# Eight units of an expert each, of 128 to 448 tokens, in place of eleven units of one or two blocks

## The chip, the core and the metric

The kernel runs on one core of a Trainium2 chip. The metric is the device time of one launch in microseconds, here the median of the runs shown. One execution was profiled; the rows below are of that execution, and the times in them count from the start of its span.

## The reference

Three stages, in float32. Attention with a window of 32 and 32 global tokens gives 2176 rows of 512 features. A router sends each row to one of 8 experts. A dense layer follows.

```python
logits = x @ w_gate                      # (2176, 512) @ (512, 8)
expert_idx = np.argmax(logits, axis=1)
for e in range(8):
    mask = expert_idx == e
    h = np.maximum(x[mask] @ w1[e], 0.0)   # 512 -> 1024
    out[mask] = gate_w[mask, None] * (h @ w2[e])   # 1024 -> 512
h = out @ w_in                           # 512 -> 2048
g = np.where(h >= 1, h, np.where(h <= -1, 0.0, (h + 1) ** 2 / 4))
result = g @ w_out                       # 2048 -> 512
```

With the reference's inputs (its default seed) the experts get 422, 331, 253, 249, 220, 149, 434 and 118 rows.

## The kernel before

Attention runs first, and the router's counts of rows come out at its end. 128 rows of expert 0 are handled early, between the router's steps, as plain float32 matmuls (`zz`: tiles `zh` and `yp`, with the raw weights `w1r`, `w2r` as an operand). Expert 0 so has 294 rows left, 2048 in all.

Those are cut into blocks of 128 rows. VectorE computes a table of blocks (`code`, `sc`, one-hot `ohh`), TensorE turns it into row numbers (`ip`, then `idx`), and POOL gathers a block's rows from DRAM by an indirect DMA (`gather`, tile `xgb`). Blocks are taken in units: eight pairs of blocks of one expert, and three single blocks, eleven units (`UNITS`, `run(list(range(11)), 0)`). With these inputs 19 blocks hold rows, and the 19 of the eleven units are always computed.

For each unit in turn:

- `x_t` turns each block on TensorE (four 128x128 transposes, tile `xTp`, pool of three banks of PSUM); ScalarE writes a rounded part (`xTh`) and VectorE the rest (`xTl`), both in F32R.
- `l1_pair` is the first layer: for each of 8 slices of the hidden layer, 4 slices of the features and 3 products of parts (`mm3`: high x high, high x low, low x high), one matmul with 256 columns, the pair's rows. 96 matmuls, tile `hp`. ScalarE and VectorE take `hp` to `hTh` and `hTl`. `l1_single` has the weights as the moving operand instead: 24 matmuls of 512 columns, after which the hidden layer is turned on TensorE too.
- `l2` is the second layer: for each block 8 x 3 matmuls of 512 columns (tile `yp`), the hidden layer as the stationary operand. ScalarE scales the block by the gate's weight and POOL scatters it to `ys` in DRAM.

The weights come in as raw float32 (`load_raw`, issued by SP), and `split_w` makes two F32R parts of each of the 8 slices: ScalarE the rounded part (`w1h`, `w2h`), VectorE the rest (`w1l`, `w2l`), 128x1024 elements each. The split of `w2` goes on during a unit's first layer, that of the next unit's `w1` during its second; a slice's next load is issued as soon as it is split. A unit whose expert is the same as the last one's skips its loads.

The order on TensorE, ScalarE, VectorE and SP is that of the code (`manual_schedule`). POOL's is chosen by the scheduler. The program branches once at the start of the units, to a path for more blocks than these:

```python
    with tc.If(slow > 22):
    ...
    block_table()
    run(list(range(11)), 0)
```

After the last unit the dense layer runs from `ys`: `y_tile` turns its rows (three of the seventeen already within the last units), then `fh` and `o` are its matmuls. Its weights are also split, in small steps (`w_step`), the first three sets during the units.

## Time and profile before

| | |
|---|---|
| median of 3 runs | 776.61 us (775.6 to 777.12) |
| profiled execution | 772.4 us, span 770.6 us |
| TensorE busy | 739.3 us, 96% |
| VectorE, ScalarE, POOL busy | 519.4, 361.2, 127.7 us |
| units of the experts | 148.86 to 374.69 us |
| dense layer | from 374.69 us |

A busy time is the sum of the stretches in which an engine had an instruction under way. Matmuls overlap in part, so a group's count times its mean duration is more than the time it holds TensorE; the distance between starts is what counts. Float32 matmuls leave two records each in the trace.

### The profile page before, as it was taken

How to read it: one execution, taken by the hardware profiler on the slowest of the kernel's cores; microseconds unless marked ns; L12 is line 12 of the kernel's file. 1: busy time of each engine (PE TensorE's matmuls, PEld its weight loads, DVE VectorE, ACT ScalarE, POOL GpSimd, SP SyncE). 2: the span in 40 equal slices, each digit the busy share in tenths (PEclk: the TensorE clock that was granted, in tenths of full speed). 3: DMA queues.
4: the chain of work that ended last, by engine and by line, in shares of the span. 5: the costliest groups of instructions: out<-in, count | busy, mean ns of one | idle time of the engine just before them, and what ended most of it. 6: DMA issues, size and time to landing. Idle time of an engine off the chain costs nothing.

```text
span 770.6 us, 16283 instructions
## 1 busy us (share of the span) xinstructions
PE 739.3 (96%) x6524; PEld 642.7 (83%) x6539; DVE 519.4 (67%) x989; ACT 361.2 (47%) x776; POOL 127.7 (17%) x164
## 2 busy tenths in 40 slices
PE   8889878999999999999999999999999999999996
PEld 4666647689899899899899899989989999999984
DVE  4778865578776866956477777757775787545443
ACT  4667653357665656754355553323432432322221
POOL 4345432242221221201100000000000000001112
PEclk9999999999999999999999999999999999999998
DMA  9677952298968966902223211110210100001111
GB/s 300 214 241 244 320 163 85 64 349 277 358 198 270 352 198 236 347 29 83 95 89 101 91 56 54 56 55 1 98 66 1 55 1 1 1 6 64 55 41 69
DMA packets 41954, 103.77 MB, mean 135 GB/s; under 512 B 6798, under 2 KB 11278, under 8 KB 39824
## 3 DMA queue, kind: packets, MB, share of 16 engines
q1 hardware_dynamic: 37312, 88.48, 34.5%
q0 software_dynamic: 4560, 14.19, 4.9%
q8 instruction: 53, 0.87, 0.5%
q14 instruction: 29, 0.24, 0.1%
HBM read 93.45 MB, written 14.18 MB: 140 GB/s over the span
## 4 chain that ended last, share of the span: by engine, by line
PE 80%; issue 7%; DMA 6%; DVE 3%; POOL 1%; SPq 0%; ACT 0%; POOLq 0%; DVEq 0%; ACTq 0%
PE fh L937 7%; PE fh L938 7%; PE fh L939 7%; PE o L938 7%; PE o L939 7%; PE o L937 7%; PE yp L939 5%; PE yp L937 5%; PE yp L938 4%; PE hp L939 4%; PE hp L938 4%; PE hp L937 4%; DMA xgb<-xs,zidx 4%; PE ps_o L300 2%; PE sp L222 2%
## 5 line engine op out<-in xcount | busy, mean ns | idle before, releaser
L1125 DVE SCALAR_TENSOR_TENSOR r<-r 128x384 f32<-128x384 f32 (+1 forms) x96 | 51.4, 536 | 119.8 <-ACT r L1124 119.6
L1127 ACT ACTIVATE gh<-g 128x384 fp32r<-128x384 f32 (+1 forms) x96 | 48.9, 509 | 125.9 <-DVE g L1126 125.9
L1124 ACT ACTIVATE r<-fh,half 128x384 f32<-128x384 f32 (+1 forms) x96 | 54.1, 564 | 114.4 <-PE fh L939 114.3
L939 PE MATMUL o<-wh,gl 128*128 128x512 f32 x272 | 107.5, 395 | 0.0
L937 PE MATMUL o<-wh,gh 128*128 128x512 f32 x272 | 107.4, 395 | 0.0
L938 PE MATMUL o<-wl,gh 128*128 128x512 f32 x272 | 107.2, 394 | 0.0
L938 PE MATMUL fh<-yl,wh 128*128 128x384 f32 (+1 forms) x320 | 104.3, 326 | 0.0
L937 PE MATMUL fh<-yh,wh 128*128 128x384 f32 (+1 forms) x320 | 104.3, 326 | 0.0
L939 PE MATMUL fh<-yh,wl 128*128 128x384 f32 (+1 forms) x320 | 104.2, 326 | 0.0
L1178 POOL DMA_INDIRECT out_dram<-acc,rid x17 | 16.5, 972 | 368.2 <-DVE acc L1176 366.7
L937 PE MATMUL hp<-xTh,w1h 128*128 128x256 f32 x256 | 72.5, 283 | 0.8 <-DVE ei L877 0.8
L939 PE MATMUL hp<-xTh,w1l 128*128 128x256 f32 x256 | 72.4, 283 | 0.0
L938 PE MATMUL hp<-xTl,w1h 128*128 128x256 f32 x256 | 72.4, 283 | 0.0
L938 PEld LDWEIGHTS fh<-yl,wh 128*128 128x128 f32 x320 | 60.0, 188 | 3.6 <-DVE rid L835 0.2
L937 PEld LDWEIGHTS fh<-yh,wh 128*128 128x128 f32 x320 | 60.1, 188 | 3.5
L939 PEld LDWEIGHTS o<-wh,gl 128*128 128x128 f32 x272 | 51.1, 188 | 12.4 <-DVE gl L1133 0.4
L937 PE MATMUL yp<-w2h,hTh 128*128 128x512 f32 x152 | 60.4, 398 | 0.0
L939 PEld LDWEIGHTS fh<-yh,wl 128*128 128x128 f32 x320 | 60.1, 188 | 0.0
L939 PE MATMUL yp<-w2h,hTl 128*128 128x512 f32 x152 | 59.6, 392 | 0.0
L938 PE MATMUL yp<-w2l,hTh 128*128 128x512 f32 x152 | 59.3, 390 | 0.0
L938 PEld LDWEIGHTS o<-wl,gh 128*128 128x128 f32 x272 | 51.1, 188 | 7.9
L937 PEld LDWEIGHTS o<-wh,gh 128*128 128x128 f32 x272 | 51.1, 188 | 7.8
(234 smaller groups left out, 1570.2 us busy)
## 6 DMA issues: line engine op xcount, KB each, us to landing
w1r<-in_w SPq DMA_DIRECT2D x44, 512.0 KB
w2r<-in_w SPq DMA_DIRECT2D x44, 512.0 KB
wraw<-in_wf SPq DMA_DIRECT2D x16, 1024.0 KB
ks<-in_k SPq DMA_DIRECT2D x16, 400.0 KB
v<-in_v SPq DMA_DIRECT2D x16, 384.0 KB
yr<-ys SPq DMA_DIRECT2D x17, 256.5 KB
qp<-in_q SPq DMA_DIRECT2D x16, 256.0 KB
xs<-xr SPq DMA_DIRECT2D x8, 512.0 KB
```

The costliest lines, as they stand in the source:

```text
L222: nc.tensor.matmul(sps[2 * c + z][a * WIN:(a + 1) * WIN, i, :], lhsT=q[r, j * WIN:(j + 1) * WIN], rhs=k_at(k, r, j), start=False, stop=(i ...
L300: nc.tensor.transpose(o[:, i, :], p[:, i, :], ident)
L937: nc.tensor.matmul(o, lhsT=ah, rhs=bh, start=first, stop=False)
L938: nc.tensor.matmul(o, lhsT=ah, rhs=bl, start=False, stop=False)
L939: nc.tensor.matmul(o, lhsT=al, rhs=bh, start=False, stop=last)
L1124: nc.scalar.activation(r[:, 0:w], o[:, 0:w], AF.Relu, bias=half, scale=0.5)
L1125: nc.vector.scalar_tensor_tensor(r[:, 0:w], r[:, 0:w], 1.0, r[:, 0:w], ALU.min, ALU.mult)
L1127: nc.scalar.activation(gh[:, 0:w], g[:, 0:w], AF.Copy)
L1178: w = nc.gpsimd.indirect_dma_start(out=out, out_offset=bass.IndirectOffsetOnAxis(ap=rid[:, tt:tt + 1].bitcast(U32), axis=0), in_=a, in_off ...
```

## The change

One unit for each expert. The experts are ranked by their number of rows (expert 0 first, then the others from the largest down), and rank k has the fixed capacity `CAPS[k]`: 320, 448, 384, 256, 256, 256, 192 and 128 rows. `ORDER` is the order in which the ranks are computed: 320, 448, 384, 128, 256, 192, 256, 256; these are units 0 to 7. Where an expert has more rows than its capacity, a new slow path (`overflow`) handles the rest after a branch.

- `l1_wide` streams a unit's whole capacity in one matmul: 96 matmuls of as many columns as the unit has rows (the unit of 128 keeps `l1_single`).
- A capacity that is no multiple of 128 has a last block of 64 rows. Its hidden layer stays in float32 (`hq`), and its second layer is 16 plain float32 matmuls of 256 columns with the raw `w2r`, on two 128x64 tiles of the array, `o[0:64]` and `o[64:128]`. That block comes first in `l2`, and `w2r` is loaded anew only after it.
- The blocks of a unit's second layer follow one another instead of alternating.
- There are five gather buffers instead of four, and `x_t` turns up to four blocks. The table has 19 entries instead of 24 and takes fewer operations. Each unit loads its weights without a condition. The buffers of wide units lie in those of the dense layer's weights, whose first loads come later.

```diff
-NB = 24
+CAPS = (320, 448, 384, 256, 256, 256, 192, 128)
+ORDER = (0, 1, 2, 7, 3, 6, 4, 5)
+BLOCKS = [(k, 128 * i, min(128, CAPS[k] - 128 * i)) for i in range(4) for k in range(8) if CAPS[k] > 128 * i]
+BLOCKS.sort(key=lambda b: (b[1] > 0, b[2] < 128))
+NB = len(BLOCKS)
+NX = 16
...
-    UNITS = []
-    for z in range(4):
-        UNITS += [(4 * z, 4 * z + 1), (4 * z + 2, 4 * z + 3), (16 + z,)]
-    UNITS += [(20,), (21,), (22,), (23,)]
+    UNITS = [[i for i, b in enumerate(BLOCKS) if b[0] == k] for k in ORDER]
+    for u in UNITS:
+        u.sort(key=lambda i: BLOCKS[i][1])
     xslot = {}
-    for j, u in enumerate(UNITS):
-        for z, i in enumerate(u):
-            xslot[i] = 2 * (j % 2) + z if j < 11 else 2 + j % 2
+    for n, i in enumerate(sum(UNITS, [])):
+        xslot[i] = (0, 1, 4, 2, 3)[n % 5]
     xg = {}
 
     def gather(i):
-        t = xgb[xslot[i]]
-        nc.gpsimd.indirect_dma_start(out=t, out_offset=None, in_=xs,
-                                     in_offset=bass.IndirectOffsetOnAxis(ap=idx[:, i:i + 1].bitcast(U32), axis=0))
+        t, r = xgb[xslot[i]], BLOCKS[i][2]
+        nc.gpsimd.indirect_dma_start(out=t[0:r], out_offset=None, in_=xs,
+                                     in_offset=bass.IndirectOffsetOnAxis(ap=idx[0:r, i:i + 1].bitcast(U32), axis=0))
         xg[i] = t
...
+    gather(UNITS[0][0])
+    gather(UNITS[0][1])
...
-    xTh, xTl = (mp.tile([128, 4, 256], F32R, name=f"xT{z}") for z in "hl")
+    xgb.append(mp.tile([128, XW], F32, name="xgb4"))
+    gather(UNITS[0][2])
+    xTn = [mp.tile([128, 4, 256], F32R, name=f"xT{z}") for z in "hl"]
+    xTw = [wp.tile([128, 1024], I64, tag="wraw", name="xTw", bufs=2).bitcast(F32R)[:, 0:4 * max(CAPS)].rearrange("p (k c) -> p k c", k=4)
+           for z in range(2)]
     hTh, hTl = (mp.tile([128, 8, 256], F32R, name=f"hT{z}") for z in "hl")
+    hTx = [wp.tile([128, 8, 128], F32R, tag=f"w{z}0", name="hTx") for z in "hl"]
+    hq = {}
...
+    def x_turn2(j, z, tag="xT"):
+        i = UNITS[j][z]
+        return turn(xg[i], tag, BLOCKS[i][2])
+
     def x_parts(j, z, p):
         i = UNITS[j][z]
-        parts(p, xTh[:, :, z * 128:(z + 1) * 128], xTl[:, :, z * 128:(z + 1) * 128])
-        V.tensor_copy(gt[xslot[i]], xg[i][:, DM:XW])
+        r = BLOCKS[i][2]
+        parts(p[:, :, 0:r], *(x[:, :, z * 128:z * 128 + r] for x in xT(j)))
+        V.tensor_copy(gt[i][0:r], xg[i][0:r, DM:XW])
+        if r < 128:
+            nc.gpsimd.tensor_copy(gt[i][r:2 * r], xg[i][0:r, DM:XW])
 
     def x_t(j):
-        for z, i in enumerate(UNITS[j]):
-            x_parts(j, z, turn(xg[i]))
+        for z in range(len(UNITS[j])):
+            x_parts(j, z, x_turn2(j, z))
 
     def mm3(o, ah, al, bh, bl, first, last):
         nc.tensor.matmul(o, lhsT=ah, rhs=bh, start=first, stop=False)
         nc.tensor.matmul(o, lhsT=ah, rhs=bl, start=False, stop=False)
         nc.tensor.matmul(o, lhsT=al, rhs=bh, start=False, stop=last)
...
-    def l1_pair(nxt):
-        for g in range(4):
-            o = ps.tile([128, 512], F32, tag="h", name="hp", bufs=3)
-            for u in range(2):
-                f = slice((2 * g + u) * 128, (2 * g + u + 1) * 128)
+    def l1_wide(j, nxt):
+        n = CAPS[ORDER[j]]
+        u = 2 if n <= 256 else 1
+        xh, xl = xT(j)
+        if halved(j):
+            hq[j] = wp.tile([128, YW], F32, tag="yr", name="yr", bufs=4)[:, 0:DM].rearrange("p (f c) -> p f c", f=8)
+            nxt = None
+        for g in range(8 // u):
+            o = ps.tile([128, 512], F32, tag="h", name="hp", bufs=3)[:, 0:u * n]
+            for v in range(u):
+                f = slice((u * g + v) * 128, (u * g + v + 1) * 128)
                 for k in range(4):
-                    mm3(o[:, u * 256:(u + 1) * 256], w1h[k][:, f], w1l[k][:, f], xTh[:, k, :], xTl[:, k, :], k == 0, k == 3)
-            h, l = (t[:, 2 * g:2 * g + 2, :].rearrange("p f c -> p (f c)") for t in (hTh, hTl))
-            nc.scalar.activation(h, o, AF.Relu)
-            V.scalar_tensor_tensor(l, o, 0.0, h.bitcast(F32), ALU.max, ALU.subtract)
-            if g:
-                split_w(2, g - 1, nxt)
+                    mm3(o[:, v * n:(v + 1) * n], w1h[k][:, f], w1l[k][:, f], xh[:, k, 0:n], xl[:, k, 0:n], k == 0, k == 3)
+            o = o.rearrange("p (f c) -> p f c", f=u)
+            e = slice(u * g, u * g + u)
+            m = n // 128 * 128
+            to = [(0, min(m, 256), hTh[:, e, 0:min(m, 256)], hTl[:, e, 0:min(m, 256)])]
+            if m > 256:
+                to.append((256, m, hTx[0][:, e, :], hTx[1][:, e, :]))
+            for a, b, h, l in to:
+                nc.scalar.activation(h, o[:, :, a:b], AF.Relu)
+            if m < n:
+                nc.scalar.activation(hq[j][:, e, :], o[:, :, m:n], AF.Relu)
+            for a, b, h, l in to:
+                V.scalar_tensor_tensor(l, o[:, :, a:b], 0.0, h.bitcast(F32), ALU.max, ALU.subtract)
+            if g * u >= 2 and g * u % 2 == 0:
+                split_w(2, g * u // 2 - 1, nxt)
...
-        o = [ps.tile([128, 512], F32, tag="y", name="yp", bufs=2) for _ in sl]
         if nxt is not None:
             for k in range(2 if len(sl) == 1 else 0, 4):
                 split_w(1, k, nxt2)
         if table:
             positions()
         ahead = nxt is not None and len(UNITS[nxt]) == 1
-        for k in range(4):
-            for z in range(2):
-                f = 2 * k + z
-                for t in range(len(sl)):
-                    c = slice(t * 128, (t + 1) * 128)
-                    mm3(o[t], hTh[:, f, c], hTl[:, f, c], w2h[k][:, z, :], w2l[k][:, z, :], f == 0, f == 7)
-            if k == 0 and 8 <= j < 11:
-                y_tile(j - 8, ps.tile([128, 4, 128], F32, tag="xT", name="xTp", bufs=3), yg, j - 8)
-            if ahead and k < 3:
-                split_w(2, k, nxt2)
-        if not ahead and len(sl) == 2:
-            w_step(5, 3)
-        for t, i in enumerate(sl):
-            g = gt[xslot[i]]
+        todo = list(enumerate(sl))
+        if halved(j):
+            todo.insert(0, todo.pop())
+        for n, (t, i) in enumerate(todo):
+            r = BLOCKS[i][2]
+            o = ps.tile([128, 512], F32, tag="y", name="yp", bufs=2)
+            for k in range(4):
+                for z in range(2):
+                    f = 2 * k + z
+                    if r == 128:
+                        mm3(o, *hT(f, t), w2h[k][:, z, :], w2l[k][:, z, :], f == 0, f == 7)
+                        continue
+                    for q in range(2):
+                        nc.tensor.matmul(o[64 * q:64 * q + 64, 0:256], lhsT=hq[j][:, f, :], rhs=w2r[k][:, z, 256 * q:256 * q + 256],
+                                         start=(f == 0), stop=(f == 7))
+                if n == 0 and k == 0 and 5 <= j < 8:
+                    y_tile(j - 5, ps.tile([128, 4, 128], F32, tag="xT", name="xTp", bufs=3), yg, j - 5)
+                if ahead and n == len(sl) - 1 and k < 3:
+                    split_w(2, k, nxt2)
+            if r < 128 and nxt is not None:
+                for k in range(4):
+                    load_raw(2, k, nxt)
+            if n == 0 and not ahead and j > 3:
+                w_step(6, 3)
+            g = gt[i]
...
+    def run():
+        js = list(range(len(UNITS)))
+        for i in UNITS[1]:
+            gather(i)
         for k in range(4):
-            split_w(1, k, None)
-        x_t(j)
-
-    def run(js, table):
-        if len(js) > 1:
-            for i in UNITS[js[1]]:
-                gather(i)
-            for k in range(4):
-                load_raw(1, k, js[1])
-        for n, j in enumerate(js):
-            nxt, nxt2 = ((js + [None, None])[n + z] for z in (1, 2))
+            load_raw(1, k, 1)
+        for j in js:
+            nxt, nxt2 = (n if n < len(UNITS) else None for n in (j + 1, j + 2))
+            single = len(UNITS[j]) == 1
+            if j == 4:
+                load_y(0)
+                load_y(1)
+            if j == 7:
+                for t in range(3, 6):
+                    load_y(t)
+            l1_single(j, nxt, nxt2) if single else l1_wide(j, nxt)
+            if nxt is not None and not single:
+                x_t(nxt)
             if nxt2 is not None:
                 for i in UNITS[nxt2]:
                     gather(i)
-            single = len(UNITS[j]) == 1
-            if j == 7:
-                load_y(0)
-                load_y(1)
-            if j == 10:
-                for t in range(3, 6):
-                    load_y(t)
-            l1_single(j, nxt, nxt2) if single else l1_pair(nxt)
-            if nxt is not None and not single:
-                x_t(nxt)
-            if j == 8:
+            if j == 5:
                 load_y(2)
-            if j == 0:
+            if j == 3:
                 while wq[0][1] is load_w:
                     f, op = wq.pop(0)
                     op(f)
-            l2(j, nxt, nxt2, j == table)
-
-    def first(j):
-        for kind in (1, 2):
+            l2(j, nxt, nxt2, j == 0)
...
+    with tc.If(slow > 0):
+        overflow()
     block_table()
-    run(list(range(11)), 0)
+    run()
     mo.close()
```

On TensorE, at the end of unit 0's first layer and the start of its second, where the rows of unit 1 are turned (`xTp` is the turned block, `xgb` the gathered one, `yr` holds the hidden layer of the half block). Before:

```order
L939 MATMUL hp<-xTh,w1l_2994 128x256
L920 MATMUL xTp<-ident,xgb_91 128x128 [waits DMASW6_49]
L920 MATMUL xTp<-ident,xgb_91 128x128 x3
L920 MATMUL xTp<-ident,xgb_92 128x128 [waits DMASW7_49]
L920 MATMUL xTp<-ident,xgb_92 128x128 x3
L937 MATMUL yp<-w2h_2995,hTh 128x512 [waits Activation_49]
L938 MATMUL yp<-w2l_2999,hTh 128x512 [waits DVE_49]
```

Now:

```order
L929 MATMUL hp<-xTw,w1l_2984 128x320
L903 MATMUL xTp<-ident,xgb_95 128x128 [waits DMASW0_49]
L903 MATMUL xTp<-ident,xgb_95 128x128 x3
L903 MATMUL xTp<-ident,xgb_96 128x128 [waits DMASW1_49]
L903 MATMUL xTp<-ident,xgb_96 128x128 x3
L903 MATMUL xTp<-ident,xgb_93 128x128 [waits DMASW4_49]
L903 MATMUL xTp<-ident,xgb_93 128x128 x3
L903 MATMUL xTp<-ident,xgb_94 128x64 [waits DMASW5_49,DVE_49]
L903 MATMUL xTp<-ident,xgb_94 128x64 x3
L1010 MATMUL yp<-w2r_89,yr 64x256 [waits DMAHW4_49]
L1010 MATMUL yp<-w2r_89,yr 64x256 x3
L1010 MATMUL yp<-w2r_90,yr 64x256 [waits DMAHW5_49]
```

Four blocks are turned instead of two, the fourth with a wait on VectorE, and the second layer starts with the float32 matmuls of the half block.

On POOL, from the first gathers to the branch at the start of the units (`TENSOR_LOAD nbi` reads the branch's condition). Before:

```order
L686 DMA xgb_89<-xs,idx 128x514 [waits DMAHW2_49,DMAHW1_49,DMAHW7_49,DMAHW0_49,DVE_49]
L686 DMA xgb_90<-xs,idx 128x514
L535 DMA ys<-y,zpos 2176x513 [waits DVE_49,Activation_49]
L1067 TENSOR_LOAD nbi [waits DVE_49]
L1069 COMPARE_AND_BRANCH
```

Now:

```order
L694 DMA xgb_93<-xs,idx 128x514 [waits DMAHW2_49,DMAHW1_49,DMAHW7_49,DMAHW0_49,DVE_49]
L694 DMA xgb_94<-xs,idx 128x514
L694 DMA xgb_2993<-xs,idx 64x514
L920 COPY gt<-xgb_2993 64x2 [waits DMASW3_49,Pool_49]
L694 DMA xgb_93<-xs,idx 128x514 [waits DMASW1_49,DVE_49,PE_49]
L694 DMA xgb_94<-xs,idx 64x514 [waits DMASW2_49,DVE_49,PE_49]
L694 DMA xgb_2993<-xs,idx 128x514 [waits DVE_49,PE_49,Pool_49]
L545 DMA ys<-y,zpos 2176x513 [waits DVE_49,Activation_49]
L920 COPY gt<-xgb_94 64x2 [waits DMASW5_49]
L1170 TENSOR_LOAD nbi [waits DVE_49]
L1172 COMPARE_AND_BRANCH
```

Two more gathers of 64 and 128 rows and one of 128 for units 1 and 2, a third one for unit 0, and two small copies now come before the branch; the gathers of unit 1's first two blocks stay behind it.

## Rows read from the trace of the kernel before

**Rows 1.** The page: busy time, share and instructions of each engine.

```profile
PE 739.3 (96%) x6524; PEld 642.7 (83%) x6539; DVE 519.4 (67%) x989; ACT 361.2 (47%) x776; POOL 127.7 (17%) x164
```

**Rows 2.** Window of the units: length, busy by engine, clock, DMA share, GB/s.

```profile
148.86:374.69 225.83, 225.01 (x1401) 202.24 (x1401) 159.44 (x228) 132.68 (x169) 47.75 (x35) 1.00 0.68 237
```

**Rows 3.** Timeline of TensorE, a pair and a single: start, length, instruction, count.

```profile
232.48 0.28 PE L937 MATMUL hp<-xTh,w1h 128*128 128x256 f32 x1
...
243.99 0.60 PE L920 MATMUL xTp<-ident,xgb 128*128 128x128 f32 x4
244.35 0.47 PE L937 MATMUL yp<-w2h,hTh 128*128 128x512 f32 x1
...
255.34 0.39 PE L937 MATMUL hp<-w1h,xTh 128*128 128x512 f32 x1
...
260.78 0.60 PE L920 MATMUL xTp<-ident,xgb 128*128 128x128 f32 x4
...
262.50 0.50 PE L937 MATMUL yp<-w2h,hTh 128*128 128x512 f32 x1
...
268.37 0.28 PE L937 MATMUL hp<-xTh,w1h 128*128 128x256 f32 x1
```

**Rows 4.** Timeline of TensorE in the dense layer, matmuls of 384 columns.

```profile
382.34 0.34 PE L937 MATMUL fh<-yg,wh 128*128 128x384 f32 x1
...
382.87 0.34 PE L937 MATMUL fh<-yg,wh 128*128 128x384 f32 x1
```

**Rows 5.** Timeline of TensorE, the early block of expert 0 in float32.

```profile
132.78 5.60 PE L522 MATMUL zh<-xzT,w1r 128*128 128x128 f32 x48
138.22 0.58 PE L739 MATMUL ip<-ohh,ohl 128*128 128x24 f16 x17
...
140.03 5.42 PE L529 MATMUL yp<-w2r,xgb 128*128 128x512 f32 x12 [0.69 <-ACT xgb L525]
145.28 1.04 PE L920 MATMUL xTp<-ident,xgb 128*128 128x128 f32 x8
```

**Rows 6.** Timeline of TensorE in attention, float32 matmuls on tiles of 32 columns.

```profile
104.19 1.07 PE L367 MATMUL lg<-xT,wg 128*32 128x512 f32 x8
105.07 0.86 PE L321 MATMUL gxb<-v,pgt 128*32 128x64 f32 x48
...
106.89 1.10 PE L345 MATMUL xo<-v,pto 128*32 128x64 f32 x64
108.15 0.38 PE L217 MATMUL sp<-mask 128*128 128x512 bf16 x1 [0.16 <-PE xo L345]
```

**Rows 7.** Timeline of TensorE, matmuls of 8 columns, new weights for each record.

```profile
126.89 0.96 PE L409 MATMUL gxb<-wg,xgT 128*128 128x8 f32 x8
127.70 0.63 PE L360 MATMUL ps_x<-ident,xr 128*128 128x128 f32 x4
```

**Rows 8.** Timeline of VectorE behind the first layer of rows 3's pair.

```profile
248.05 0.69 DVE L925 TENSOR_TENSOR xTl<-xTp,xTh 128x512 fp32r<-128x512 f32 x1
...
248.72 4.63 DVE L870 TENSOR_TENSOR w1l<-w1r,w1h 128x1024 fp32r<-128x1024 f32 x4
```

**Rows 9.** Timelines of VectorE, POOL and TensorE at the units' start; landing of gathers.

```profile
132.96 0.17 DVE L705 TENSOR_TENSOR ci<-gxb,cst 128x8 int32<-128x8 f32 x1 [0.38 <-PE gxb L461]
...
137.32 0.58 DVE L735 TENSOR_TENSOR ohh<-phi,sc 128x408 f16<-128x408 int32 x1
...
140.64 0.95 POOL L686 DMA_INDIRECT xgb<-xs,idx  x1 [0.30 <-issue]
...
DMA to landing us min/median/max: 3.4/4.5/5.5
...
148.86 0.39 PE L937 MATMUL hp<-xTh,w1h 128*128 128x256 f32 x1 [0.82 <-DVE ei L877]
...
161.88 0.66 PE L920 MATMUL xTp<-ident,xgb 128*128 128x128 f32 x4 [0.81 <-DMA xgb<-xs,idx]
```

**Rows 10.** DMA from 138 to 200 us, GB/s in 40 equal slices.

```profile
GB/s 0 13 188 143 16 0 0 21 191 103 301 420 418 420 346 350 328 145 322 340 351 375 399 416 407 420 404 302 48 160 190 140 370 194 227 408 420 418 412 386
```

More of the change, by code (lines that the diff above doesn't have):

```diff
@@ L67 @@
 COFF, CW = _const_layout()
-CP = 1
+CP = 1 + NB + 2 * E
 def _constants():
@@ L88, in _constants @@
     first = (ee == 0).astype(np.float32)
[L89 to L96 removed]
+    put("key", (E - 1 - ee - 8 * 4096 * ee + (1 << 20) * first).astype(np.float32)[None])
+    put("nsub", (4096 * ee + 128 * first).astype(np.float32)[None])
+    put("code", (32 * ee + first).astype(np.float32)[None])
+    slot, off, rows = (np.array(x, np.float32) for x in zip(*BLOCKS))
+    put("slot", slot[None])
+    put("sub", off[None])
+    put("cod", ((32 * ee + first)[None, :] + off[:, None] / 128).astype(np.float32).reshape(1, -1))
+    put("cap", np.array(CAPS, np.float32)[None])
+    put("capb", np.array([x // 128 * 128 for x in CAPS], np.float32)[None])
+    put("half", np.array([x % 128 for x in CAPS], np.float32)[None])
+    put("pcol", p.astype(np.float32))
     return c
@@ L976, in l1_single @@
             if nxt is not None and z < len(UNITS[nxt]):
-                px.append(turn(xg[UNITS[nxt][z]], "xT" if z == 0 else "h"))
+                px.append(x_turn2(nxt, z, "xT" if z == 0 else "h"))
             ph.append(turn(hs[z]))
@@ new lines, in l2 @@
+        if halved(j):
[22 more added lines that the diff above has]
+            g = gt[i]
+            y = mp.tile([128, YW], F32, tag="y", name="y", bufs=3)
+            if r == 128:
+                nc.scalar.activation(y[:, 0:DM], o, AF.Copy, scale=g[:, 0:1])
+            else:
+                for q in range(2):
+                    h = slice(64 * q, 64 * q + 64)
+                    nc.scalar.activation(y[0:64, 256 * q:256 * q + 256], o[h, 0:256], AF.Copy, scale=g[h, 0:1])
+            V.tensor_copy(y[0:r, DM:YW], g[0:r, 1:2])
+            nc.gpsimd.indirect_dma_start(out=ys, out_offset=bass.IndirectOffsetOnAxis(ap=cpos[0:r, i:i + 1].bitcast(U32), axis=0),
+                                         in_=y[0:r], in_offset=None, bounds_check=N - 1, oob_is_err=False)
```

277 lines of the change are left out of this document (151 added, 126 removed).

## The prediction

> **What bounds the kernel now.** I read the page's shares of the engines first: TensorE is busy for 96% of the span [rows 1]. An average doesn't say which stage can give time back, so next comes the window of the stretch that the change touches. From the first matmul of the experts (148.86 us) to the first of the dense layer (374.69 us) TensorE is busy for 225.01 of 225.83 us, at a granted clock of 1.00, the upper of its two levels (2.4 GHz); VectorE has 159 us of work in it and ScalarE 133, and the DMA engines are 0.68 busy [rows 2]. This stretch is a plain queue of matmuls, so its length is their number times their spacing. The reader should take the spacing from one start to the next, not the printed duration, since matmuls overlap.
>
> The timeline gives the spacings. A pair's first layer, 96 matmuls of 256 columns, runs from 232.48 to 243.99: 11.51 us, 0.1199 each. Its second layer, two blocks of 24 matmuls of 512 columns, takes 244.35 to 255.34, so 5.50 a block. A single unit's first layer is 24 matmuls of 512 columns from 255.34 to 260.78, 5.44 us or 0.2267 each; four turns follow (1.72 us), and its second layer takes 5.87 to the next unit [rows 3]. A turn is 0.36 to 0.43 us; I use 0.4. With 384 columns, three matmuls of the dense layer take 0.53 us, 0.1767 each [rows 4].
>
> Before, the stretch holds 8 pairs and 3 singles: first layers 8 x 11.51 + 3 x 5.44 = 108.4 us, second layers 16 x 5.50 + 3 x 5.87 = 105.6, the rest (turns, one wait) 225.8 - 214.0 = 11.8.
>
> **The first layer of the eight units.** By the inputs of the reference the tokens fit every capacity, so the overflow branch isn't taken. Each unit but the single one issues 96 matmuls, as wide as its capacity. 320 and 448 columns lie midway between measured widths: 0.148 and 0.202 each, 14.2 and 19.4 us. 384 columns give 17.0, three units of 256 give 34.5, the single one 5.4.
>
> The unit of 192 is unknown: no matmul of this kind (F32R operands) with fewer than 256 columns is in the trace. Going on down the straight line through 384 and 256 gives 0.092 (8.8 us). But every matmul loads 128 columns of new weights first, and where only 8 columns are streamed, eight records still take 0.81 us, 0.101 each [rows 7]: a load that the stream no longer covers. So 9.7 us at least by that row, and 11.5 if it is no quicker than 256 columns. I take the middle, 10.6, and keep 8.8 and 11.5; a far worse price is a rival below. Sum of first layers: 101.1, a gain of 7.3.
>
> The Trainium skill, "TensorE: Matmul & The Clock Gate", section "LDWEIGHTS (loading the stationary operand)", prices a load by its columns over 1.2 GHz: an estimate of 0.107 for 128, which would make this unit 10.2 us and the forecast 762.3, where the row's floor makes them 9.7 and 761.8. Row and page agree within 6%, and both speak against a gain in proportion to the columns.
>
> **The second layer.** 16 blocks are full: 15 x 5.50 + 5.87 = 88.4 us. Three half blocks each issue 16 fp32 matmuls of 256 columns instead of 24, on two halves of the array's columns. What does fp32 cost? The first expert's early block shows it: 24 matmuls (48 records) of 128 columns from 132.78 to 138.22 are 0.227 each, and six (12 records) of 512 from 140.03 to 145.28 are 0.875 [rows 5]; 256 columns lie a third of the way, 0.443. Do column tiles run side by side? Four matmuls of 512 columns on 128x32 tiles take from 104.19 to 105.07, 0.88 us, as long as one alone; and 32 of 64 columns, with new weights each, are done in 1.26 us with 0.16 idle, so 0.137 for each four against 0.119 on the fp32 line [rows 6]. So at most 0.02 is lost a step. A half block is 8 steps x 0.443 = 3.54 at best, 3.7 with that loss; I take 3.6. Changing the tiling may cost something: the row behind the tiled matmuls waits 0.16 [rows 6], so up to 1.0 for six changes is kept as a bound. Sum: 88.4 + 10.8 = 99.2, a gain of 6.4.
>
> **Turns and the new wait.** The steps on the path are now 16 blocks turned (0.4 each) less the early ones, four turns for the single unit, three y tiles: 1.6 + 1.2 + 0.4 + 1.7 + 2.4 + 1.2 = 8.5, a gain of 3.3, since two singles go with their extra turns and the old 0.81 wait at 161.88 [rows 9] isn't counted.
> But x_t for the unit of 448 turns four blocks in a pool of three banks: the fourth must wait until VectorE has read the first. In the pair shown VectorE's read of a turned block starts at 248.05 and takes 0.69, so it ends 4.75 us after the first layer [rows 3, 8], behind two weight splits. In the wide unit one of the two splits sits before the last group, so I take 1.1 us off: 3.65. Three turns last 1.25 us, the wait is 2.4. Bounds: 0 and 3.5. Behind it on TensorE stands the whole second layer, which nothing else covers.
>
> **The start.** x_t(0) gets a third block, whose gather follows the second's (140.64) on POOL, at some 141.9, and lands 3.4 to 5.5 us later [rows 9], at 145.3 to 147.4; TensorE comes to it at about 146.2 [rows 5]. With a turn of 0.4 the first matmul, now at 148.86, moves by about 0.7; bounds 0 and 2. The first gathers for the second unit are issued behind the branch in both kernels, but a copy and three other gathers now stand ahead of the branch on POOL. The second unit is turned at 149.6 + 14.2 = 163.8 now, 2 us later than the turn that waited until 161.88, which should cover that; without it a wait like the old 0.81 [rows 9] comes back.
>
> **What I cost at nothing.** The block table takes VectorE from 132.96 to 137.90 [rows 9], and about a third of it goes (four operations of 256 to 272 elements fall to 64 to 152). But TensorE has the 48 early records in front of `ip`, up to 138.22 [rows 5], and starts `ip` with no wait; without that cover the gain would be some 1.6 us. Weights: one set of 4.2 MB for each unit; at the 400 GB/s of the busy slices [rows 10] a set takes 10.5 us, and the shortest unit lasts 13. Where a half block keeps w2r, the next load is issued later; the tightest is unit 5 of 192 tokens, where two sets queue from its second layer on and are wanted 15 to 20 us later. The evacuations are cut smaller, but ScalarE and VectorE fall from 11 x 8 to 8 x 8 splits. The dense layer is unchanged.
>
> **The sum.** -7.3 - 6.4 - 3.3 + 2.4 + 0.7 = -13.9 us. The profiled execution lasted 772.4 us (span 770.6 and 1.8 around it), so 758.5; the median of the runs shown is 4.2 above it, 776.6, so I forecast **762.7**. The likeliest case's own range adds the bounds: best -1.8 - 0.2 - 2.4 - 0.7 (757.6), worst +0.9 + 1.3 + 1.1 + 1.3 (767.3); with 0.7 for the spread of the runs, 757 to 768.
>
> **Rivals.**
> 1. The 192-column matmuls fall to the fp32 rate. Nothing in the trace shows this kind so narrow; the nearest row of such width is the fp32 one [rows 5], which at 192 columns is 0.335: 32.1 us for the unit instead of 10.6, and the time is 784, slower. It decides from 0.255 each on. Against it: 256 columns already run at 0.1199, and the column line has no step down to there. Chance 0.13.
> 2. The two halves of the array take turns. Then a half block is 16 x 0.443 = 7.1, +10.5 in all: 773. Against it stand four tiles in the time of one [rows 6]. Chance 0.07.
> 3. VectorE falls behind in unit 5 (192 tokens): eight splits at 1.16 each [rows 8] are 9.3 us; hidden parts, two blocks' parts, a y tile and six steps of dense weights are some 10 more, in 21 us of matmuls. What is late next is w1l for unit 6, up to 5 us: 767.7. Against it: in the pair shown w1l was done at 253.35, 2 us before TensorE wanted it at 255.34 [rows 3, 8]. Chance 0.09.
> 4. The half blocks' weight loads lie open: half of 0.101 [rows 7] for 64 columns, 32 records a block, 1.6 us, 4.9 in all: 767.6. The tiled row with at most 0.02 a step [rows 6] speaks against it. Chance 0.04.
>
> The Trainium skill states rival 4 as a rule: "TensorE: Matmul & The Clock Gate", Part 3, under "The mechanism", lets loads overlap running matmuls only when their row groups differ, and both halves here use all rows. The tiled rows of this trace, all rows too, don't bear it out.
>
> **How the numbers follow.** The likeliest case has 0.66, and 0.01 is left for losses that just cancel the gain. 757 to 773.5 takes in the likeliest and rivals 2 to 4, together 0.86; rival 1 stays outside. About 0.2% (1.5 us) is what a measurement of this kernel can tell from no change. Faster 0.86, same 0.01, slower 0.13.
>
> **What the profile after would show.** The stretch from first expert matmul to first dense one should last about 211 us. Right or wrong by step: spacing of the 192-column matmuls near 0.11; a half block in 3.6 us, its two outputs starting within a few ns; one idle spot of 2 to 3 us ahead of the second unit's last turn, released by VectorE; first expert matmul at about 149.6; `ip` still at 138.2. The prediction is wrong if the 192 spacing is near 0.33, if halves alternate, or if TensorE shows waits for splits or w2r in units 4 to 6.

## The result, and the profile after

The changed kernel takes 764.99 us (median of 4 runs, 764.29 to 768.41) against 776.59 for the kernel before on the same chip (4 runs, 775.6 to 777.12): the ratio is 0.9861, with a 95% interval from 0.983 to 0.9892. The forecast was 762.7, in 757.0 to 773.5. On the medians 11.6 us were gained, where the sum had 13.9. The profiled execution of the changed kernel lasted 764.29 us (span 762.5), so between the two profiled executions the gain is only 8.1; an experiment below shows where the other part went.

The page after. TensorE has 10.6 us less to do than in [rows 1], and VectorE 34 less:

```profile
PE 728.7 (96%) x6388; PEld 627.6 (82%) x6403; DVE 485.5 (64%) x955; ACT 338.6 (44%) x793; POOL 127.8 (17%) x167
```

The windows of the changed kernel come next, with the columns of [rows 2]. The first row is the whole stretch from the first matmul of the experts to the first of the dense layer, the others are single stages of it. In this order they are the first unit's first layer, the same with the turns behind it, the first unit's half block, its two full blocks, the single unit's first layer, a first layer of 256 columns, that of the unit of 192, and the dense part to the end of the span:

```profile
152.26:366.10 213.84, 212.19 (x1261) 185.38 (x1261) 125.44 (x200) 109.77 (x185) 46.21 (x36) 1.00 0.61 208
152.26:167.45 15.19, 14.32 (x96) 14.06 (x97) 6.36 (x10) 7.16 (x20) 4.39 (x6) 1.00 0.66 218
152.26:170.37 18.11, 16.46 (x113) 15.66 (x113) 8.92 (x15) 9.22 (x23) 4.39 (x6) 1.00 0.58 194
...
170.37:173.97 3.60, 3.60 (x34) 2.21 (x32) 3.60 (x8) 3.60 (x6) 2.92 (x2) 1.00 0.24 73
173.97:185.27 11.30, 11.30 (x50) 9.13 (x49) 4.51 (x14) 2.20 (x4) 6.37 (x4) 1.00 0.95 323
...
261.12:266.72 5.60, 5.60 (x26) 4.46 (x25) 4.68 (x5) 4.15 (x5) 0.58 (x1) 1.00 0.96 322
...
274.40:285.61 11.21, 11.21 (x97) 11.20 (x96) 4.32 (x5) 4.38 (x6) 1.20 (x2) 1.00 0.74 264
...
297.83:308.53 10.70, 10.70 (x98) 10.70 (x96) 4.85 (x9) 5.65 (x11) 1.50 (x2) 1.00 0.61 231
...
366.10:762.50 396.40, 387.41 (x2025) 349.73 (x2023) 257.40 (x449) 143.56 (x250) 17.48 (x18) 0.99 0.14 49
```

The stretch fell from 225.83 us [rows 2] to 213.84, where about 211 was forecast. The stages show what was right at once. The half block takes 3.60 us, as forecast, and the unit of 192 takes 10.70, or 0.111 a matmul (forecast 10.6). They also show what was not right: two full blocks take 11.30 us, 5.65 each, where 5.50 was carried over from [rows 3]; the single unit's first layer takes 5.60 instead of 5.44; and a first layer of 256 columns takes 11.21, less than the 11.51 of [rows 3]. The same instructions thus cost something else than before, at the same granted clock of 1.00.

The timelines of the start, of TensorE, VectorE and POOL in this order, answer to [rows 5] and [rows 9]:

```profile
140.20 0.58 PE L730 MATMUL ip<-ohh,ohl 128*128 128x19 f16 x17
...
147.27 1.43 PE L903 MATMUL xTp<-ident,xgb 128*128 128x128 f32 x12
...
152.26 0.38 PE L927 MATMUL hp<-xTw,w1h 128*128 128x320 f32 x1 [1.65 <-PEq L1172]
...
167.45 0.66 PE L903 MATMUL xTp<-ident,xgb 128*128 128x128 f32 x4 [0.87 <-DMA xgb<-xs,idx]
168.77 1.67 PE L903 MATMUL xTp<-ident,xgb 128*128 128x128 f32 x12 [0.66 <-DMA xgb<-xs,idx]
170.37 3.67 PE L1010 MATMUL yp<-w2r,yr 128*64 128x256 f32 x32
...
169.24 0.68 DVE L908 TENSOR_TENSOR xTw<-xTp,xTw 128x512 fp32r<-128x512 f32 x1
...
156.28 0.18 POOL L920 COPY gt<-xgb 64x2 f32<-64x2 f32 x1 [1.39 <-DMA xgb<-xs,idx]
163.69 1.24 POOL L694 DMA_INDIRECT xgb<-xs,idx  x1 [7.23 <-ACT yr L953]
165.23 0.95 POOL L694 DMA_INDIRECT xgb<-xs,idx  x1 [0.30 <-issue]
```

Three things stand here. `ip` comes 2.0 us later than in [rows 5], although nothing of the change runs ahead of it on TensorE. TensorE idles 1.65 us at the branch (0.82 in [rows 9]). And ahead of the second unit's half block the waits that are named are those for two gathers, 0.87 and 0.66 us, not one for VectorE. POOL issues these two gathers at 163.69 and 165.23, 7.23 us after its last copy ahead of the branch, and they land some 3.4 us later. In the kernel before, POOL's first gather behind its branch came sooner:

```profile
154.28 0.98 POOL L686 DMA_INDIRECT xgb<-xs,idx  x1 [4.19 <-DVE hTl L950]
```

### The profile page after: what moved, and what is told of

The parts are those of the page before. It is cut to its first block, busy times and chain, and to the rows that moved or that the text cites. A ratio compares the mean times of both kernels' runs of the same rounds, so it can differ in the third digit from the quotient of the medians.

```text
span 762.5 us, 15859 instructions
## 1 busy us (share of the span) xinstructions
PE 728.7 (96%) x6388; PEld 627.6 (82%) x6403; DVE 485.5 (64%) x955; ACT 338.6 (44%) x793; POOL 127.8 (17%) x167
## 4 chain that ended last, share of the span: by engine, by line
PE 71%; issue 6%; POOL 1%; DVE 1%; ACT 0%; POOLq 0%; DVEq 0%
PE fh L927 7%; PE fh L928 7%; PE fh L929 7%; PE o L928 7%; PE o L929 7%; PE o L927 7%; PE hp L927 4%; PE hp L929 4%; PE hp L928 4%; PE yp L927 4%; PE yp L929 4%; PE yp L928 4%; PE yp L1010 1%; POOL out_dram L1270 1%; PE xTp L903 1%
## 5 line engine op out<-in xcount | busy, mean ns | idle before, releaser
L955 DVE SCALAR_TENSOR_TENSOR hTl<-hp,hTh 128x256 fp32r<-128x256 f32 (+1 forms) x40 | 20.1, 504 | 55.2 <-ACT yr L953 32.0
L257 ACT ACTIVATE p<-sp,mn 128x128 f32<-128x128 f32 x128 | 45.4, 373 | 20.9 <-DVE mn L242 12.8
L1218 DVE TENSOR_TENSOR g<-r,fh 128x384 f32<-128x384 f32 (+1 forms) x96 | 51.0, 532 | 3.3
L1225 DVE TENSOR_TENSOR gl<-g,gh 128x384 fp32r<-128x384 f32 (+1 forms) x96 | 50.7, 528 | 0.0
L878 DVE TENSOR_TENSOR w2l<-w2r,w2h 128x1024 fp32r<-128x1024 f32 x32 | 38.8, 1224 | 15.6 <-ACT w2h L877 15.6
L1268 DVE TENSOR_TENSOR acc<-o,acc 128x512 f32<-128x512 f32 x68 | 44.5, 682 | 2.7 <-PE o L929 2.7
```

Of the source, the lines that this page charges most:

```text
L257: nc.scalar.activation(p[:, i, :], sp[:, i, :], AF.Exp, bias=mn[:, i:i + 1], scale=scale, accum_out=ss[b][:, i, h:h + 1])
L878: V.tensor_tensor(l[k], r[k], h[k].bitcast(F32), ALU.subtract)
L1218: nc.vector.tensor_tensor(g[:, 0:w], r[:, 0:w], o[:, 0:w], ALU.max)
L1225: nc.vector.tensor_tensor(gl[:, 0:w], g[:, 0:w], gh[:, 0:w].bitcast(F32), ALU.subtract)
L1268: nc.vector.tensor_tensor(a, o, a, ALU.add)
```

## The experiments

The kernel before, run beside them, took 775.85 us in the median of six runs (experiments 1, 2, 4 and 5; a seventh run lasted 2538.97 and is left out), 775.42 (6 and 7) and 774.4 (3, 8 and 9).

**1. Where the buffer stands (e_phase).** The change adds a fifth gather buffer of 2080 bytes between the weight tiles and the x and h tiles. The tiles' addresses in the two programs suggested a theory.

```diff
-    xgb.append(mp.tile([128, XW], F32, name="xgb4"))
-    gather(UNITS[0][2])
     xTn = [mp.tile([128, 4, 256], F32R, name=f"xT{z}") for z in "hl"]
...
     hTh, hTl = (mp.tile([128, 8, 256], F32R, name=f"hT{z}") for z in "hl")
+    xgb.append(mp.tile([128, XW], F32, name="xgb4"))
+    gather(UNITS[0][2])
```

> In the changed kernel a full block of a second layer takes 5.64 us (72 matmuls 16.92, 48 matmuls 11.30) where rows of before gave 5.50, and a single unit's first layer 5.60 instead of 5.44; a 256-column first layer takes 11.2 instead of 11.51. The new fifth gather buffer of 2080 bytes stands between the weight tiles and the x and h tiles, so the addresses of those two groups, which agreed modulo 4096 bytes in the kernel before, no longer do. This kernel has the same tiles with that buffer behind the h tiles, so that they agree again; nothing else changes. Theory 1 (address): a full block falls back to 5.50, the single first layer to 5.44, the 256-column first layers rise to 11.5; with 18 full blocks less 2.5 us and three 256-column units plus 0.9 us, about 1.5 us less in all. Theory 2 (a block now keeps one PSUM bank for 24 matmuls in a row): no figure moves by more than 0.03 us a block, and the time stays within 0.5 us.

The windows of this kernel: the first unit's two full blocks, the single unit's first layer, a first layer of 256 columns, and two full blocks of the unit after the single one.

```profile
172.57:183.60 11.03, 11.03 (x50) 9.12 (x49) 4.60 (x14) 2.33 (x4) 4.14 (x3) 1.00 0.96 349
...
258.86:264.33 5.47, 5.47 (x26) 4.46 (x24) 4.68 (x5) 4.13 (x5) 0.57 (x1) 1.00 0.95 312
...
271.89:283.41 11.52, 11.52 (x97) 11.51 (x96) 4.41 (x5) 4.37 (x6) 1.32 (x2) 1.00 0.78 287
284.33:295.34 11.01, 11.01 (x50) 9.12 (x49) 10.69 (x14) 7.35 (x9) 5.63 (x1) 1.00 0.87 268
```

All three figures are those of [rows 3] again: 5.5 a block, 5.47, 11.52. Theory 1 holds: the place of a small buffer moves the spacing of matmuls that never touch it, up for one shape and down for another. The kernel took 762.12 us (761.5 to 766.8, ratio 0.9839, interval 0.979 to 0.9888); its stretch is 212.75 us, 1.1 shorter than that of the changed kernel. The 1.5 that was expected counted 18 full blocks; there are 16, which take 88.8 us in all against 90.7 in the changed kernel, and the third blocks of the wide units stay at 5.6.

**2. Pairs of blocks in turn (e_alt).** The full blocks of a unit alternate every three matmuls, as before.

```diff
...
-                        mm3(o, *hT(f, t), w2h[k][:, z, :], w2l[k][:, z, :], f == 0, f == 7)
+                        for tt, ii in part:
+                            mm3(banks[ii], *hT(f, tt), w2h[k][:, z, :], w2l[k][:, z, :], f == 0, f == 7)
```

> The full blocks of a second layer are taken in pairs again, three matmuls of one block and three of the other, as in the kernel before; addresses stay as in the changed kernel. Theory 2 (bank): a full block falls from 5.64 to 5.50 us, a pair from 11.30 to 11.0, about 2 us less in all. Theory 1 (address): a pair stays at 11.3 us. In either case a pair behind a half block may wait some tenths of a us for the half block's bank.

The window of the two full blocks behind the unit that follows the single one:

```profile
290.80:302.10 11.30, 11.30 (x51) 9.12 (x49) 10.97 (x14) 7.35 (x9) 5.63 (x1) 1.00 0.88 276
```

The figure is the same, so Theory 2 falls. The kernel took 768.81 us (one run): in the pairs of the wide units TensorE now waits for banks, 0.67 us at the first and 2.01 at the second, and these units' second layers are 4.0 us longer.

**3. What the address must agree in (e_pad).** The buffer is made 32 bytes longer.

```diff
-    xgb.append(mp.tile([128, XW], F32, name="xgb4"))
+    xgb.append(mp.tile([128, 528], F32, name="xgb4")[:, 0:XW])
```

> The fifth gather buffer is 2112 bytes instead of 2080, nothing else is changed. The h and x tiles then stand 64 bytes off a multiple of 2048 from the weights (in the changed kernel 32 bytes), and all of them at 32 bytes off a multiple of 64. Theory 1a (what counts is the difference of the two addresses modulo 64): full blocks at 5.50 us, three blocks 16.5, 256-column first layers at 11.5. Theory 1b (the difference modulo 2048 or 4096): as in the changed kernel, 5.64 and 11.2. Theory 1c (each tile's own address modulo 64): 5.64 too or more, since the weights are off now as well.

Two full blocks of the first unit, and a first layer of 256 columns:

```profile
175.26:186.56 11.30, 11.30 (x50) 9.09 (x49) 3.12 (x13) 1.63 (x3) 3.59 (x3) 1.00 1.01 377
...
275.37:286.68 11.31, 11.31 (x97) 11.30 (x96) 4.35 (x5) 4.37 (x6) 1.20 (x2) 1.00 0.78 280
```

Full blocks stay at 5.65, so 1a falls. 1b and 1c both forecast that, and neither names the 11.31 of the first layer, which lies between 11.21 and 11.51. The first layers of 448 and 384 columns, 19.71 and 16.97 us in the changed kernel, take 19.58 and 16.85 here, so they too hang on the place. Which property of the address decides stays open. The time was 765.55 us (one run).

**4. The two halves of a half block (e_serial).** All matmuls of the left half first, then all of the right half.

```diff
                     for q in range(2):
-                        nc.tensor.matmul(o[64 * q:64 * q + 64, 0:256], lhsT=hq[j][:, f, :], rhs=...)
+                        for g in (2 * f % 8, 2 * f % 8 + 1):
+                            if f // 4 == q:
+                                nc.tensor.matmul(o[64 * q:64 * q + 64, 0:256], lhsT=hq[j][:, g, :], rhs=...)
```

> In the half blocks all eight matmuls of the left column half run first and then all eight of the right one, instead of in turn; in the changed kernel a half block takes 3.60 us and the two tiles of a pair start 6 to 7 ns apart. Theory (the two array halves work at the same time, which is where 3.60 comes from): each half block takes twice as long, about 7.1 us, and the three together 10.5 us more: about 775 us for the kernel. Rival (the two halves are served one after the other anyway and 3.60 is simply the cost of 32 matmuls): a half block stays at 3.60 us and the time within 0.5 us.

The windows of the first two half blocks:

```profile
169.69:176.69 7.00, 7.00 (x33) 4.30 (x32) 6.68 (x14) 4.28 (x6) 4.88 (x4) 0.89 0.69 201
...
209.11:215.35 6.24, 6.24 (x33) 3.92 (x32) 5.92 (x11) 5.71 (x8) 2.44 (x3) 1.00 0.17 44
```

TensorE's records within a half block, over the same length of time: first the left half alone (this kernel), then both halves in turn (the changed kernel).

```profile
209.59 2.11 PE L1012 MATMUL yp<-w2r,yr 128*64 128x256 f32 x9
```

```profile
206.65 2.11 PE L1010 MATMUL yp<-w2r,yr 128*64 128x256 f32 x18
```

At full clock (the second window) the half block takes 6.24 us, against 3.60 in turn. So the halves do work at the same time, and this is worth 2.6 us a half block; the first window has a granted clock of 0.89 and is longer for that. In 2.11 us the two halves in turn get through 18 records and one half alone through 9. A record lasts 0.38 us, so alone the records start (2.11 - 0.38) / 8 = 0.216 us apart: a matmul, which leaves two records, costs 0.43 us alone, near the 0.443 of the forecast, and two of them in turn cost no more. The 7.1 us that were expected aren't reached because the edit doesn't part the halves wholly: the first four records of the right half run beside the last four of the left one. The kernel took 772.24 us (one run).

**5. What the narrow capacities are worth (e_whole).**

```diff
-CAPS = (320, 448, 384, 256, 256, 256, 192, 128)
+CAPS = (384, 448, 384, 256, 256, 256, 256, 128)
```

> Capacities 384 and 256 instead of 320 and 192 for the first and the seventh rank: two of the three half blocks are whole again, everything else as changed. Theory, from durations of the changed kernel: the first unit's first layer rises from 14.32 to 16.96 us (the 384-column one), its half block from 3.60 to 5.64; the other unit's first layer from 10.70 only to 11.2, its half block from 3.60 to 5.64. Sum +7.2 us, of which the 192-column first layer is worth 0.5 us only. Rival (192 columns saves as the columns say, 0.227 x 64 / 512 us for each of 96 matmuls, 2.7 us): +9.4 us.

The first layer of the unit that had 192 columns, and the first unit's first layer:

```profile
307.99:319.20 11.21, 11.21 (x97) 11.21 (x96) 6.16 (x9) 5.80 (x8) 1.02 (x1) 1.00 0.71 258
...
156.11:174.67 18.56, 18.56 (x96) 18.53 (x97) 7.09 (x17) 6.71 (x17) 3.70 (x5) 0.91 0.71 236
```

11.21 against 10.70: a quarter fewer columns saves 0.5 us, not quite 5%. The rival, a saving in proportion, would have had 2.7. The first unit took 18.56 instead of 16.96, since the clock fell here (below). The kernel took 776.17 us (one run), 4 more than expected, most of it the later start of this execution and the fallen clock.

**6. What ends last ahead of the second unit (e_early, e_turnh, e_both).** Two edits, alone and together: the overflow's x tile moves to the fifth buffer, so that the second unit's first gathers may be issued ahead of the branch; and the fourth turn gets a bank of the first layer's tag.

```diff
-            x = xgb[2 + j % 2]
+            x = xgb[4]
...
-            x_parts(j, z, x_turn2(j, z))
+            x_parts(j, z, x_turn2(j, z, "xT" if z < 3 else "h"))
```

> Between the last first-layer matmul of the first unit (about 166.4) and its half block (170.37) the changed kernel shows two DMA waits (0.87 and 0.66 us) and then the fourth turn, which starts when VectorE ends an xTw copy. The two late gathers go into buffers that the overflow branch also uses, so GpSimd issues them only behind the branch, at 163.69 and 165.23. Here the overflow's x tile is the fifth buffer, and all four gathers are issued ahead of the branch. Theory (VectorE ends last): the two DMA waits go, the fourth turn still waits for VectorE, and the span from the first first-layer matmul to the half block stays at 18.1 us within 0.3. Rival (the DMA ends last): it falls by about 1.5 us.

> The fourth turn of the second unit takes a PSUM bank of the first layer's tag, so that it waits for no copy of VectorE; the gathers stay where they are in the changed kernel. Theory (both waits overlap, the DMA one ends at 168.8, VectorE's at 169.9): only the part that sticks out goes, 0.2 to 0.4 us less between the first first-layer matmul and the half block. Rival (VectorE's wait is the whole 2.4 us that was forecast for it): 2.2 us less.

> Both edits together: gathers ahead of the branch and the fourth turn in a bank of the first layer's tag. Theory: with neither wait left the four turns take about 1.8 us from 166.4 on, and the half block starts about 2.0 us earlier (first first-layer matmul to half block about 16.1 instead of 18.1 us). Rival: a third wait (the half block's own tiles, evacuated by ScalarE at 167.1) takes their place and less than 1 us is gained.

Windows from the first first-layer matmul to the half block (18.11 us in the changed kernel): with the gathers early, with the turn in the other bank, with both.

```profile
151.73:169.85 18.12, 16.03 (x113) 15.72 (x113) 9.08 (x15) 9.24 (x23) 4.01 (x5) 1.00 0.57 183
```

```profile
153.99:172.05 18.06, 16.39 (x112) 15.66 (x112) 8.72 (x15) 9.02 (x23) 4.70 (x6) 1.00 0.60 198
```

```profile
152.95:168.91 15.96, 15.95 (x112) 15.72 (x112) 6.92 (x12) 7.92 (x21) 3.49 (x5) 1.00 0.64 207
```

And TensorE's waits for its turns, of the first edit alone and then of the second alone:

```profile
PE xTp L903 <- DVE xTw L908: 2.1, 1, 2.1
```

```profile
PE xTp L903 <- DMA xgb<-xs,idx: 1.7, 2, 0.9
```

Each edit alone gains nothing, 18.12 and 18.06 against 18.11, and both together gain 2.15. With the gathers early, the wait for VectorE stands there in full, 2.1 us; with the turn in the other bank, the two waits for gathers do. In the changed kernel the waits lie over each other: the second wait for a gather ends at 168.77, and VectorE ends its copy at 169.92. Of the three expectations the one for the turn alone was a little too high. With both edits the kernel took 763.6 us (762.42 to 765.45, ratio 0.9845, interval 0.981 to 0.988); the two single ones 763.58 and 765.96 (one run each).

**7. The branch (e_short).**

```diff
-        for j in range(NX):
+        for j in range(2):
             x = xgb[2 + j % 2]
```

> The overflow branch's body handles 2 blocks instead of 16 (work that these inputs do not use), everything else as changed; the branch is not taken. The changed kernel shows 1.65 us of idle TensorE at the branch where the kernel before shows 0.82, and its body is some 2.5 times longer on TensorE. Theory (the idle time grows with the code that is jumped over): back to about 0.8 us. Rival (it is the joining of the engines, whatever the length): stays at 1.65 us within 0.2. Also looked at: GpSimd's way through the branch, 7.2 us in the changed kernel.

POOL's first gather behind the branch, from its timeline, TensorE's wait, and windows from the branch on:

```profile
160.40 1.01 POOL L694 DMA_INDIRECT xgb<-xs,idx  x1 [1.91 <-ACT yr L953]
```

```profile
PE hp L927 <- PEq L1172: 1.9, 1, 1.9
```

```profile
154.00:156.00 2.00, 1.51 (x10) 1.54 (x11) 0.00 (x0) 0.00 (x0) 1.39 (x3) 1.00 0.79 181
156.00:158.00 2.00, 2.00 (x10) 2.00 (x9) 0.42 (x1) 0.50 (x2) 0.90 (x1) 0.51 0.88 320
158.00:160.00 2.00, 2.00 (x11) 2.00 (x10) 0.00 (x0) 0.18 (x1) 0.18 (x1) 0.64 0.97 328
```

TensorE's idle time didn't fall: 1.9 us, so the theory is wrong for TensorE. POOL's way through did get shorter, 1.91 us instead of 7.23, so the late gathers come from the length of the body. The kernel was slower all the same (767.93 us, one run): behind the idle spot the granted clock fell to 0.51, which cost some 1.5 us, and `ip` came at 142.22 in this execution, 2.0 us later than in the first profile of the changed kernel.

**8. Both kernels once more (before2, after2).**

> The kernel before once more, for its start. In its first profile the table's matmul stood at 138.22 us and the time was 772.4, 4.2 below the median; in the profiles of the changed kernel and its variants it stands anywhere from 139.3 to 143.3. Theory (executions differ there whatever the kernel): this profile shows it at 139 to 142 us and the branch idle above 0.82 us. Rival (the changed kernel's constants delay its start): 138.2 within 0.4 us again.

> The changed kernel once more. Theory: the stretch from the first first-layer matmul to the dense part is 213.8 us within 0.4 again, the table's matmul anywhere from 139 to 143 us, and the idle at the branch anywhere from 1.1 to 2.2. Rival (the start is a property of the kernel): 140.2 us and 1.65 us within 0.3 again.

TensorE's timeline at the table's matmul and the first matmul of the experts, and the window of the stretch, first of the kernel before:

```profile
139.89 0.58 PE L739 MATMUL ip<-ohh,ohl 128*128 128x24 f16 x17
...
150.86 0.36 PE L937 MATMUL hp<-xTh,w1h 128*128 128x256 f32 x1 [1.16 <-DVE ei L878]
```

```profile
150.86:376.59 225.73, 224.99 (x1400) 202.22 (x1401) 159.22 (x226) 132.51 (x169) 45.63 (x35) 1.00 0.68 237
```

then of the changed one:

```profile
146.66 0.58 PE L730 MATMUL ip<-ohh,ohl 128*128 128x19 f16 x17
...
158.56 0.38 PE L927 MATMUL hp<-xTw,w1h 128*128 128x320 f32 x1 [1.50 <-PEq L1172]
```

```profile
158.56:372.65 214.09, 212.12 (x1260) 185.38 (x1261) 125.38 (x200) 109.64 (x185) 41.69 (x36) 1.00 0.61 208
```

The stretch is the same within 0.3 us in each kernel, 225.83 and 225.73, 213.84 and 214.09. What comes ahead of it is not: `ip` stands at 138.22 and 139.89 in the kernel before, at 140.20 and 146.66 in the changed one, and from 139.2 to 143.3 in its variants. The 146.66 lies beyond the 143 that was expected. For this last execution the granted clock tells most of it, in the windows ahead of `ip`, first of the second profile of the kernel before, then of the second of the changed one:

```profile
0.00:100.00 100.00, 84.27 (x2310) 59.01 (x2311) 71.75 (x197) 60.70 (x279) 43.56 (x83) 1.00 0.83 260
100.00:138.00 38.00, 32.34 (x747) 25.15 (x746) 24.61 (x94) 17.69 (x70) 14.16 (x24) 0.96 0.37 111
```

```profile
0.00:100.00 100.00, 84.43 (x2249) 58.57 (x2249) 66.95 (x188) 57.96 (x264) 43.52 (x83) 0.97 0.77 245
100.00:138.00 38.00, 30.04 (x741) 21.79 (x742) 23.07 (x75) 18.77 (x83) 13.01 (x23) 0.87 0.47 147
```

The difference in clock, 0.03 of 100 us and 0.09 of 38, makes an estimate of 6.4 us, and its `ip` is 6.8 later. So executions differ in the attention stage by more than the 2.0 us by which the first profile after came late. From `ip` to the first matmul of the experts it is 10.64 and 10.97 us before and 12.06 and 11.90 after. That the changed kernel's `ip` is later by a little on the whole isn't excluded by two profiles of the kernel before; 2.0 us as a rule would leave a gain of only 8.1 of the stages' 10.1 (the sum below), just outside the interval of the medians, 8.4 to 13.2. The times were 774.31 and 770.87 us (one run each).

**9. What helps, together (e_best).** The two edits of experiment 6, with the h tiles ahead of the fifth buffer and the x tiles behind it.

```diff
+    hTh, hTl = (mp.tile([128, 8, 256], F32R, name=f"hT{z}") for z in "hl")
     xgb.append(mp.tile([128, XW], F32, name="xgb4"))
     gather(UNITS[0][2])
     xTn = [mp.tile([128, 4, 256], F32R, name=f"xT{z}") for z in "hl"]
...
-    hTh, hTl = (mp.tile([128, 8, 256], F32R, name=f"hT{z}") for z in "hl")
```

> Gathers ahead of the branch, the fourth turn in a bank of the first layer's tag, and the h tiles ahead of the fifth gather buffer with the x tiles behind it, so that the h tiles keep the weights' address modulo 4096 and the x tiles do not. Theory: full blocks from the two h tiles at 5.50 us (16 blocks, 2.2 us less; the two blocks from the third h tile stay at 5.6), 256-column first layers stay at 11.2 and the single one at 5.60, first first-layer matmul to half block 16.0 instead of 18.1: the stretch from the first first-layer matmul to the dense part 213.8 - 2.2 - 2.1 = 209.5 us, about 760.7 for the kernel against 764.99 of the changed one. Rival (the 256-column first layers hang on the h tiles' place too): they rise to 11.5, and 0.9 us of it is lost.

The window of the stretch, then the first unit's two full blocks, the single unit's first layer and a first layer of 256 columns:

```profile
150.99:360.79 209.80, 209.80 (x1261) 185.35 (x1261) 125.33 (x200) 109.42 (x185) 44.04 (x35) 1.00 0.62 212
...
170.54:181.57 11.03, 11.03 (x50) 9.12 (x49) 6.42 (x15) 3.26 (x5) 8.06 (x4) 1.00 0.84 270
...
256.83:262.42 5.59, 5.59 (x25) 4.46 (x24) 4.69 (x5) 4.15 (x5) 0.71 (x1) 1.00 0.93 313
269.98:281.19 11.21, 11.21 (x98) 11.21 (x97) 4.33 (x5) 4.38 (x6) 1.33 (x2) 1.00 0.73 269
```

The stretch is 209.80 us (expected 209.5), TensorE busy in all of it. The full blocks and the first layers of 256 columns have the better of their two figures; the single unit's first layer stays at 5.59, as expected, where experiment 1 had 5.47. The kernel took 759.31 us (757.61 to 759.96, 6 runs) against 774.4, a ratio of 0.9807, interval 0.9779 to 0.9836: the fastest version of this study.

## Why the prediction was right, step by step

- **First layers**, 101.1 forecast: 100.9 measured (14.3 without the wait behind it, 19.7, 17.0, 5.6, 3 x 11.2, 10.7). The 192-column price, the boldest guess, was 10.6 and is 10.70; the 8.8 us of the straight line through 384 and 256 columns is refuted, as are the fp32 rate (rival 1) and, by experiment 5, a larger worth of the narrow unit. The Trainium skill, "TensorE: Matmul & The Clock Gate", section "LDWEIGHTS (loading the stationary operand)", gives an estimate of 0.107 for a load of 128 columns; the 0.111 measured agrees with a load that sets the pace, but no run here took the load by itself. The sum is close partly by errors that cancel: three units of 256 columns cost 0.3 us less each, and 448 columns 0.3 more, the single unit 0.2 more.
- **Second layers**, 99.2 forecast: two of the half blocks were right to the hundredth (3.60), and the third, with a y tile turned in its middle, took 3.76 without that turn; so rivals 2 and 4 fall. The rule that the Trainium skill states for rival 4 ("TensorE: Matmul & The Clock Gate", Part 3, "The mechanism", where it excepts loads into a background weight buffer) isn't borne out as the prediction read it: the two halves use the same rows, and 16 matmuls (32 records) take 3.60 us with 2.21 us of weight loads inside them. No run here tells whether these loads fall under the exception. The term that was mis-sized is the full block: 5.50 was read from [rows 3] and applied to tiles that the change moves by 2080 bytes from the weights. The 16 full blocks took 90.7 us instead of 88.4, and all second layers 101.7, 2.5 more than forecast. Experiment 1 shows that the buffer's place is the cause of 1.9 of these 2.3, since its 16 full blocks take 88.8.
- **Turns and the new wait**, 8.5 + 2.4 forecast: 11.25 measured with the y tiles. The wait on VectorE is there, 2.1 us, but it was named only when the gathers were early: the prediction held that these gathers were covered, and they were not, since POOL needs 7.2 us for the branch (4.2 in the kernel before). By luck both waits share one place, and the sum wasn't hurt.
- **The start**, +0.7 forecast: +3.4 between the two profiled executions. Of these 2.0 lie ahead of the change's work, in the attention stage, where executions differ by as much (experiment 8). The rest, about 1.2 us from `ip` to the first matmul on the mean of the two profiles of each kernel, is the third turn (0.48: from the first transpose to the next matmul 1.35 against 0.87) and an idle spot at the branch that is some 0.6 longer. In the eleven profiles of kernels with this branch the spot is 1.1 to 2.2 us, in the two of the kernel before 0.8 and 1.2.
- **What was costed at nothing** cost nothing: `ip` waits for no table, the loads of weights are on time, and VectorE doesn't fall behind in unit 5 (rival 3): TensorE names no other wait in the stretch. But the dense part, which isn't changed, takes 396.40 and 396.45 us in the changed kernel and 395.91 in both profiles of the one before; why stays open.
- **The sum**: -11.8 for the stretch (mean of two profiles of each kernel), +1.2 for the start and +0.5 for the dense part, so -10.1 in place of -13.9; the medians say -11.6, with -13.2 to -8.4 by the interval. The forecast of 762.7 was 2.3 us too low by the medians and 3.8 by the stages. Of the 3.8 the full blocks are 2.3, the start and the dense part 0.5 each and the turns some 0.4; that the full blocks' part equals the miss of the medians is chance.

## What to carry to other kernels

A spacing read from a trace belongs to the tiles' places as well as to the shape: when a change allocates a tile ahead of others, keep their relative addresses, or read the spacing again. A removed wait is worth only what no other wait covers, so try the suspected ones alone and together. With 128 columns of new weights for each matmul, cutting the streamed columns from 256 to 192 gives back not quite 5%; a half block on the two halves of the array side by side costs 64% of a full one.

## What the runs showed of the hardware that was not expected

- F32R matmuls of 512 columns take 0.227 or 0.235 us each (5.5 or 5.64 a block of 24), and those of 256 columns 0.117, 0.118 or 0.120, as the tiles are placed; the shape that gains and the shape that loses are different ones. Neither the bank order (experiment 2) nor the clock (1.00 in all these rows) has to do with it. Why is open.
- The two halves of the array work at once on fp32 matmuls of 64 columns each: in 2.11 us the two in turn get through 18 records and one alone through 9, so two matmuls cost the 0.43 us of one (experiment 4).
- The granted clock fell to 0.51, the lower of the two levels (1.2 GHz), behind idle spots of TensorE of 1.9 us (experiment 7) and 2.2 us (experiment 5) at the branch, and cost 1.5 and 1.6 us; behind idle spots of 1.65 us and less at the same place it stayed at 1.00. It also fell (to 0.50) at the second unit's turns in experiments 3 and 4, where TensorE had waited 1.7 and 1.6 us in two spots for the gathers. But the same two waits, 1.5 to 2.0 us together, left it at 1.00 in both profiles of the changed kernel, in experiments 1 and 2 and in the second kernel of 6, and one wait of 2.1 us there left it at 1.00 in the first kernel of 6. So the length of a wait alone doesn't tell whether the clock falls.
- POOL's way past a branch that isn't taken took 7.2 us with a body for 16 blocks and 1.9 with a body for 2; TensorE's idle spot, 1.9 us with the short body (one run) and 1.1 to 2.2 with the long one, shows no gain from the shorter body.
